# A conditioned transformer block on one core: paired DMA transpositions, fewer waits, and a new instruction order

## The chip, the cores and the metric

The kernel runs on one core of a Trainium2 chip. The core has a matrix engine (TensorE, PE in the profile), three engines for elementwise work (VectorE or DVE, ScalarE or ACT, GpSimd or POOL), a queue engine (SyncE or SP) and 16 DMA engines that all queues share. The metric is device time in microseconds (us) of one launch, lower is better. The times quoted for a kernel are the median of several runs.

## What is computed

The input x has 2048 rows of 640 features. A conditioning row c gives six vectors (two shifts, two scales, two gates) through one matrix product. The block is an attention over a sliding window of 256 keys with 32 heads of 20 features, then a gated MLP of width 1536, each behind a layer norm that is scaled and shifted, and each added to its input through a gate:

```python
def _A_ref(x, wqkv, wo):
    qkv = (x @ wqkv).reshape(B, S, 3, H, Dh)      # S = 2048, H = 32, Dh = 20
    scores = einsum('bhqd,bhkd->bhqk', q, k) * Dh ** (-0.5)
    mask = (i - j >= 0) & (i - j < 256)
    o = einsum('bhqk,bhkd->bhqd', softmax(where(mask, scores, -1e9)), v)
    return o.reshape(B, S, D) @ wo                # D = 640
def _B_ref(x, w_gate, w_up, w_down):
    return (sigmoid(x @ w_gate) * (x @ w_up)) @ w_down

sa, ca, ga, sb, cb, gb = (silu(c) @ w_mod).reshape(6, D)
x = x + ga * _A_ref(layernorm(x) * (1 + ca) + sa, wqkv, wo)
x = x + gb * _B_ref(layernorm(x) * (1 + cb) + sb, w_gate, w_up, w_down)
```

Inputs, weights and result are bf16.

## The kernel before

The 2048 rows are cut into 8 chunks of 256 rows, and a chunk into two blocks of 128. For each chunk the kernel runs these stages.

- `ln1` (L874): the statistics and the normalised rows `x` of both blocks, then their transposition into the tile `hT` (features on the partitions), then the scale and shift of `modulate` (L813). Chunks 0 and 1 are transposed on PE (`pe_transposes`, L831, for chunks below `NPH` = 2), the others by DMA (`transp_dma`, L808), one DMA of 128x640 for each block.
- `qkv` (L917): for each block, Q and then K are projected on PE (five matmuls of 320 columns for each half of the features) and copied by ACT or DVE out of PSUM into a staging tile `stg` of 128x1024, in which each head has 32 columns. The staging tile is then transposed into `QT` or `KT`. For chunks below `NPQ` = 2 PE does that, as matmuls with the identity (`M<-ident,stg` in the profile, four for each half) and a second copy out of PSUM; for the others one DMA transposition does it for each block and each of Q and K. There are four staging tiles. V is projected last.
- `attention` (L1175): for each half of the heads, sets of score matmuls into the one PSUM tile `S`, an exponential on ACT from `S` into `E`, masks on POOL, and one burst of matmuls of `E` with V, then a normalisation on DVE.
- `outproj` (L1213): the product with wo, the residual, the second layer norm, and its transposition into `h2T`, by DMA for all chunks, one DMA for each block.
- `mlp` (L1261): gate and up matmuls over `h2T` with 256 columns, a tanh on ACT, the product on DVE, then the down matmuls and the store.

The stages of different chunks are interleaved. While the weights are loaded (all through the same DMA queues, over the first quarter of the run) the conditioning vectors are made by small matmuls (`silubc` in the profile).

The order of all work is written out in `PLAN` (L353), a table of one number for each operation: the operation's place in the recording, and its engine. `Prog.schedule` (L151) walks the table, gives each operation to its engine in that order, and picks the buffer for each tile. `Prog.emit` (L262) then finds for each operation the semaphores that it must wait for. An operation waits for each operation that it depends on, also where an earlier wait of the same engine, or a wait that the awaited operation itself had made, already implies that it has ended. It skips a semaphore only where the same engine has waited for that value itself.

So each engine runs a fixed list. If the head of a list waits, everything behind it on that engine waits too. The DMA transpositions are all issued by SP.

Of the kernel before, what the change touches and what calls it, by code (L numbers as in the profile page):

```python
# [13 lines left out]
D = 640  # L14
H = 32
DH = 20
# [35 lines left out]
class Tile:  # L52
# [18 lines left out]
    @property  # L71
    def ap(self):
        return self.pool.aps[self.slot]

# [6 lines left out]
class Prog:  # L81
# [180 lines left out]
    def emit(self):  # L262
# [26 lines left out]
        for e in ENGS:  # L289
            cnt = 0  # L290
            for o in self.order[e]:
                if o.isdma:
                    continue
                if o.signal:
                    cnt += 1
                    o.key, o.val = e, cnt
        handles = {}
# [10 lines left out]
        with nc.Block() as block:  # L308
            for e in ENGS:
# [4 lines left out]
                def body(engine, ops=ops, e=e):  # L314
                    seen = {}
                    for o in ops:
                        w = {}
                        for d in need[o]:
                            if seen.get(d.key, 0) < d.val and w.get(d.key, 0) < d.val:
                                w[d.key] = d.val  # L320
                        for k, v in w.items():
                            engine.wait_ge(h(k), v)
                            seen[k] = v
# [5 lines left out]
                    if e == "sp":  # L329
                        for k, v in finals.items():  # L330
                            if seen.get(k, 0) < v:
# [17 lines left out]
def c_pe(n):  # L349
# [1026 lines left out]
```

## Time and profile before

| | |
|---|---|
| three runs | 324.90, 325.63 and 331.31 us; median 325.63 us |
| the profiled execution | 323.86 us, of which 321.8 us are the span from the first to the last instruction; 2.06 us lie around it |
| granted PE clock | 1.000 |
| busiest engines | PE 315.8 us, ACT 213.6 us, DVE 198.6 us, POOL 189.0 us |
| DMA | 32.96 MB in 62127 packets, of which 45946 are under 512 bytes |

The profile gives times as starts within the span and as durations. Matmuls overlap: a row's duration of one matmul is longer than the step from it to the next. The profile's step is therefore read from the starts of rows that follow each other. An arrow `<-` in brackets names what ended an idle time.

### The profile page before, as it was taken

To read this page: it belongs to the slowest core of one execution; us is meant where nothing else is said; L and a number is where in the kernel's file an instruction comes from. 1 tells how busy PE (TensorE), PEld (TensorE's weight loads), DVE (VectorE), ACT (ScalarE), POOL (GpSimd) and SP (SyncE) were. 2 spreads that over 40 slices of the span, in tenths; PEclk is the share of its full clock that TensorE was granted. 3 is DMA by queue.
4 is the path that set the end of the run, shared out by engine and by line. 5 is a ranking of instruction groups with operands and counts; after the bars stand their busy time and mean duration, and the time that the engine had idled before them with its cause. 6 is when DMAs were issued, how large, how long until landed. Compare 5 with 4: busy or idle time off the path is not lost.

```text
span 321.8 us, 11856 instructions
## 1 busy us (share of the span) xinstructions
PE 315.8 (98%) x5045; PEld 236.9 (74%) x5045; DVE 198.6 (62%) x424; ACT 213.6 (66%) x229; POOL 189.0 (59%) x349
## 2 busy tenths in 40 slices
PE   7999999999999999999999999999999999999997
PEld 2677667677877777766777677877877777877885
DVE  4689897877886756584555555465534474386323
ACT  2699897876787986768686867676976746411220
POOL 4338759778768483948484848577575826601000
PEclk9999999999999999999999999999999999999999
DMA  7989999999912534226327200220800006002101
GB/s 232 350 269 287 219 182 237 207 223 306 202 29 43 88 77 55 44 63 108 77 22 92 51 22 3 65 42 25 132 16 4 22 22 104 22 2 61 44 0 44
DMA packets 62127, 32.96 MB, mean 102 GB/s; under 512 B 45946, under 2 KB 60794, under 8 KB 62074
## 3 DMA queue, kind: packets, MB, share of 16 engines
q1 hardware_dynamic: 59904, 29.73, 43.5%
q10 hardware_dynamic: 2170, 2.46, 2.4%
q8 instruction: 40, 0.66, 0.9%
q14 instruction: 13, 0.11, 0.1%
HBM read 18.68 MB, written 2.62 MB: 66 GB/s over the span
## 4 chain that ended last, share of the span: by engine, by line
PE 93%; DMA 3%; DVE 1%; ACT 1%; issue 0%; ACTq 0%; DVEq 0%
PE M L686 77%; PE S L687 8%; PE M L687 7%; DMA hT<-x 2%; DMA x<-in_A_x_dram 1%; PE S L686 1%; ACT hT L819 1%; DVE st L781 1%; PE S L678 0%; DVE x L803 0%; ACT stg L902 0%; DVE KT L903 0%; ACTq L572 0%; DVE st L783 0%; ACT hT L902 0%
## 5 line engine op out<-in xcount | busy, mean ns | idle before, releaser
L1055 ACT ACTIVATE E<-S 128x2048 bf16<-128x2048 f32 x56 | 105.1, 1876 | 41.7 <-PE S L687 38.7
L1060 POOL TENSOR_SCALAR_AFFINE_SELECT E<-E 128x256 bf16<-128x256 bf16 x112 | 46.4, 424 | 57.4 <-ACT E L1055 24.6
L1064 POOL TENSOR_SCALAR_AFFINE_SELECT E<-E 128x512 bf16<-128x512 bf16 x112 | 70.3, 643 | 4.6 <-DVE x L803 1.2
L686 PE MATMUL M<-h2T,wg 128*128 128x256 bf16 x480 | 67.0, 273 | 0.0
L686 PE MATMUL M<-h2T,wu 128*128 128x256 bf16 x480 | 66.7, 273 | 0.0
L1277 DVE SCALAR_TENSOR_TENSOR hh<-sig,M 128x512 bf16<-128x512 f32 x48 | 32.4, 677 | 42.9 <-ACT sig L1275 25.2
L686 PE MATMUL M<-wd,hh 128*128 128x320 bf16 (+2 forms) x396 | 57.0, 295 | 0.0
L686 PEld LDWEIGHTS M<-h2T,wg 128*128 128x128 bf16 x480 | 45.4, 98 | 7.7 <-DVE T L1150 0.2
L686 PEld LDWEIGHTS M<-h2T,wu 128*128 128x128 bf16 x480 | 45.2, 98 | 7.3
L1275 ACT ACTIVATE sig<-M 128x512 f32<-128x512 f32 x48 | 28.5, 595 | 31.5 <-PE M L686 31.2
L686 PEld LDWEIGHTS M<-wd,hh 128*128 128x128 bf16 x396 | 37.2, 98 | 13.6 <-DVE hh L1277 0.2
L1033 POOL TENSOR_SCALAR_AFFINE_SELECT E<-E 128x1024 bf16<-128x1024 bf16 x28 | 31.9, 1145 | 4.7 <-ACT E L1029 3.2
L687 PEld LDWEIGHTS S<-QT,KT 20*64 20x64 bf16 (+1 forms) x1856 | 20.0, 100 | 17.0 <-issue 9.1
L687 PE MATMUL S<-QT,KT 20*64 20x256 bf16 (+5 forms) x1856 | 32.3, 228 | 0.1
L1029 ACT ACTIVATE E<-S 128x2048 bf16<-128x2048 f32 x14 | 26.3, 1876 | 7.2 <-PE S L687 7.1
L781 DVE BATCH_NORM_STATS2 st<-x 128x6 f32<-128x320 bf16 x64 | 28.9, 480 | 1.9 <-DMA x<-in_A_x_dram 1.5
L1150 DVE STREAM_TRANSPOSE T<-M 128x512 f32<-128x512 f32 x32 | 21.5, 700 | 13.3 <-PE S L687 11.7
L686 PE MATMUL M<-wk,hT 128*128 128x320 bf16 x160 | 27.9, 299 | 0.0
L1296 DVE TENSOR_TENSOR x<-M,x 128x320 bf16<-128x320 f32 (+2 forms) x33 | 15.4, 476 | 18.8 <-PE M L686 18.6
L686 PE MATMUL M<-wq,hT 128*128 128x320 bf16 x160 | 26.2, 299 | 0.6 <-DVE hT L820 0.5
L686 PE MATMUL M<-wv,hT 128*128 128x320 bf16 x160 | 26.1, 299 | 0.0
L686 PE MATMUL M<-wo,oT 128*128 128x320 bf16 x160 | 25.9, 299 | 0.0
(84 smaller groups left out, 356.7 us busy)
## 6 DMA issues: line engine op xcount, KB each, us to landing
x<-in_A_x_dram SPq DMA_DIRECT2D x18, 160.0 KB, 3.5
wd<-in_w_mod_dram SPq DMA_DIRECT2D x6, 320.0 KB, 5.4
wd<-in_B_w_down_dram SPq DMA_DIRECT2D x4, 480.0 KB, 5.6
wu<-in_w_mod_dram SPq DMA_DIRECT2D x5, 320.0 KB, 4.5
x<-in_A_x_dram ACTq DMA_DIRECT2D x8, 160.0 KB, 2.6
out_dram<-x SPq DMA_DIRECT2D x8, 160.0 KB, 1.9
wu<-in_B_w_up_dram SPq DMA_DIRECT2D x2, 576.0 KB, 5.6
wg<-in_B_w_gate_dram SPq DMA_DIRECT2D x2, 576.0 KB, 6.2
```

Of the source, the lines that this page charges most:

```text
L686: return e.matmul(o, l, r, start=st, stop=sp, skip_group_check=True)
L687: return e.matmul(o, l, r, start=st, stop=sp, tile_position=tp, skip_group_check=True)
L781: A("dve", lambda e, g, bi=bi, j=j: e.bn_stats(v(bi * 12 + j * 6, 6), src[bi].ap[:, j * 320:(j + 1) * 320]), 0.48, reads=[src[bi].r()], wr ...
L1029: A("act", lambda e, eng: e.activation(cell().rearrange("p m (x c) -> p m x c", c=64)[:, :, 0:4:3, :], Sp.ap[:].rearrange("p j (k x c) -> ...
L1033: A("pool", lambda e, eng, c0=c0, pat=pat, base=base, cm=cm: e.affine_select(cell()[:, :, c0:c0 + 64], cell()[:, :, c0:c0 + 64], pattern=p ...
L1055: A("act", lambda e, eng: e.activation(part(0, 512), Sp.ap[:], ACT.Exp, scale=SM_SCALE), 1.876, reads=[Sp.r()], writes=[E.r("C"), E.r("B") ...
L1060: A("pool", lambda e, eng, hc=hc, src=src, far_h=far_h: e.affine_select(side(hc), part(src, 64), pattern=[[0, 4], [-1 if far_h else 1, 64] ...
L1064: A("pool", lambda e, eng, c0=c0, near=near: e.affine_select(part(c0, 128), part(c0, 128), pattern=[[0, 4], [1 if near else -1, 128]], com ...
L1150: A("dve", lambda e, g, h=h: e.transpose(T1.ap[:, 512 * h:512 * h + 512], X[h].ap), 0.694, reads=[X[h].r()], writes=[T1.r(h)], prio=3.5, t ...
L1275: A("act", lambda e, g, pg=pg, sg=sg: e.activation(sg.ap[:], pg.ap[:], ACT.Tanh, scale=0.5), c_act(512), reads=[pg.r()], writes=[sg.r()], ...
L1277: A("dve", lambda e, g, pu=pu, sg=sg, f0=f0: e.scalar_tensor_tensor(out=hh.ap[:, f0:f0 + 2, :], in0=sg.ap[:].rearrange("p (a b) -> p a b", ...
L1296: A("dve", lambda e, g, ps=ps, bi=bi, c0=c0, n=n: e.tensor_tensor(x1[bi].ap[:, c0:c0 + n], ps.ap[:, 0:n], x1[bi].ap[:, c0:c0 + n], op=ALU. ...
```

## The change

Four things are changed together.

**One transposition for a pair.** The two normalised blocks of a chunk now lie side by side in one tile of 128x1280, and one DMA transposes both; the tiles `hT` and `h2T` change their layout from feature tile, row to block, feature tile, row. Q and K of a block lie side by side in one staging tile of 128x2048, and one DMA transposes both into a joint tile `QK`. The number of DMA transpositions of `hT` goes from 12 to 6, of `h2T` from 16 to 8.

**Chunk 1.** `NPQ` goes from 2 to 1: Q and K of chunk 1 are transposed by DMA (one DMA for each block), and PE's 32 identity matmuls for them and their eight copies out of PSUM go. The transposition of chunk 1's `hT` stays on PE (`NPH` is 2 as before). Q and K have 14 DMA transpositions after, 24 before.

**Buffers.** `x0` and `x2` (before 4 and 2 tiles of one block) become one pool of 3 tiles of a pair. `hT` and `h2T` (2 and 2) become one pool of 4. Staging is 2 tiles of 2048 columns instead of 4 of 1024. `QT` (3) and `KT` (4) become 4 joint tiles. The row of c uses a part of the tile `mt`.

**Waits and order.** `emit` now follows the plan with what each engine knows to have ended, through the waits of the operations that it waited for as well, and leaves out a wait that follows from others. Instructions that only wait, counted in the two built programs, go from 174 to 14 on ACT, from 170 to 56 on DVE, from 89 to 62 on PE, from 89 to 26 on POOL and from 78 to 19 on SP. `PLAN` is a new table throughout; more of the loads may be issued by ACT. One line of it:

```diff
-    119, 53, 76, 3, 8, 297, 86, 84, 300, 305, 333, 270, 277, 99, 281, 48, 442, 335, 28, 437, 447, 94, 13, 287, 422, 427,
...
-NPQ = 2
-PQ = ()
+NPQ = 1
...
+class Part:
+    def __init__(self, tile, i, view):
+        self.tile, self.i, self.view = tile, i, view
+    def r(self, key=None):
+        return self.tile.r((self.i, key))
+    @property
+    def ap(self):
+        return self.view(self.tile.ap, self.i)
...
+        for code in PLAN:
+            o = self.ops[code // 5]
+            known = seen[o.eng]
+            last = {}
+            for d in need[o]:
+                if known.get(d.key, 0) < d.val and (d.key not in last or last[d.key].val < d.val):
+                    last[d.key] = d
+            waits[o] = {k: d.val for k, d in last.items()
+                        if not any(x is not d and after[x].get(k, 0) >= d.val for x in last.values())}
+            for d in last.values():
+                for k, v in after[d].items():
+                    known[k] = max(known.get(k, 0), v)
+            after[o] = dict(known)
...
-    p_x0 = sbpool("x0", 4, [128, D])
-    p_x2 = sbpool("x2", 2, [128, D])
+    p_x0 = p_x2 = sbpool("x0", 3, [128, 2 * D])
...
-    p_hT = sbpool("hT", 2, [128, NDT, CH])
-    p_h2 = sbpool("h2T", 2, [128, NDT, CH])
-    p_stg = sbpool("stg", 4, [128, 1024])
-    p_QT = sbpool("QT", 3, [128, NG, CH])
-    p_KT = sbpool("KT", 4, [128, NG, CH])
+    p_hT = p_h2 = sbpool("hT", 4, [128, 2, NDT, 128])
+    p_stg = sbpool("stg", 2, [128, 2048])
+    p_QK = sbpool("QK", 4, [128, 2 * NG, CH])
...
-            turned[a] = [transp_dma(lambda bi=bi: t.ap[:, :, bi * 128:(bi + 1) * 128], lambda bi=bi: src[bi].ap[:], 4, 0.29,
-                                    [src[bi].r()], [t.r(("t", bi))], 1.42, f"atr{a}") for bi in range(2)]
+            turned[a] = [transp_dma(lambda: t.ap[:].rearrange("p b k c -> p (b k) c"), lambda: src[0].tile.ap[:], 4, 2 * TRH,
+                                    [src[bi].r() for bi in range(2)], [t.r(("t", bi)) for bi in range(2)], 1.45, f"atr{a}")]
...
-                else:
-                    transp_dma(lambda dst=dst, bi=bi: dst.ap[:, :, bi * 128:bi * 128 + 128], lambda s=s: s.ap[:], 3, 0.87,
-                               [s.r(0), s.r(1)], [dst.r((bi, 0)), dst.r((bi, 1))], 1.45, f"qkt{a}")
+            if a >= NPQ:
+                transp_dma(lambda bi=bi: qk.ap[:, :, bi * 128:bi * 128 + 128], lambda sqk=sqk: sqk.ap[:], 3, 2 * TRQ,
+                           [sqk.r((n, h)) for n in range(2) for h in range(2)],
+                           [qk.r((n, (bi, h))) for n in range(2) for h in range(2)], 1.55, f"qkt{a}")
...
-            for bi in range(2):
-                transp_dma(lambda bi=bi: h2.ap[:, :, bi * 128:(bi + 1) * 128], lambda bi=bi: x2[bi].ap[:], 2, 0.29,
-                           [x2[bi].r()], [h2.r(("t", bi))], 1.42, f"btr{a}")
+            transp_dma(lambda: h2.ap[:].rearrange("p b k c -> p (b k) c"), lambda: x2[0].tile.ap[:], 2, 2 * TRH,
+                       [x2[bi].r() for bi in range(2)], [h2.r(("t", bi)) for bi in range(2)], 1.45, f"btr{a}")
...
                 pairs = [(lambda kt=kt, i=i, ps=ps, w=w, f0=f0: (
-                    ps.ap[:, i * CH:(i + 1) * CH], w[:, kt, (f0 + i) * 128:(f0 + i + 1) * 128], h2.ap[:, kt, :]))
+                    ps.ap[:, i * CH:(i + 1) * CH].rearrange("p (b c) -> p b c", b=2), w[:, kt, (f0 + i) * 128:(f0 + i + 1) * 128],
+                    h2.ap[:, :, kt, :]))
```

The last lines show that the MLP's moving operand is now read as two pieces of 128 columns instead of one of 256. In the listings below, `M` and `S` are PSUM tiles, a name with a digit is one buffer of a pool, and the helper line that records a matmul is L686 or L687 before and L712 or L713 after.

**PE, from the first attention burst to the first scores of chunk 1.** Before, the identity matmuls that turn chunk 1's Q and K (`M<-ident,stg`) stand between the other work up to the first scores of the chunk (the first row with 64x256):

```order
L686 MATMUL M<-ident,stg 128x128 x8
L687 MATMUL S<-QT,KT 128x128 x16
L686 MATMUL M<-ident,stg 128x128 x4
L686 MATMUL M<-wk,hT 128x320 x5
L686 MATMUL M<-wv,hT 128x320 x7
L686 MATMUL M<-ident,stg 128x128 x4
L687 MATMUL S<-QT,KT 64x256 x8
L687 MATMUL S<-QT,KT 64x192 x8
L687 MATMUL S<-QT,KT 64x64 x8
L686 MATMUL M<-ident,stg 128x128 x4
```

After, the last projection of chunk 1's second Q ends three matmuls and one set of eight score matmuls ahead of these rows (the three are the last `M<-wq,hT` of chunk 1), and the last row is the first use of chunk 1's `QK`:

```order
L712 MATMUL M<-wv,hT 128x320 x13
L713 MATMUL M<-wu,silubc 32x160 x40
L713 MATMUL M<-E,V 32x256 x16
L713 MATMUL M<-E,V 32x128 x16
L713 MATMUL S<-QK 128x128 x16
L712 MATMUL M<-wv,hT 128x320 x5
L712 MATMUL M<-wq,hT 128x320 x2
L712 MATMUL M<-wk,hT 128x320 x2
L712 MATMUL M<-wq,hT 128x320 x5
L712 MATMUL M<-wk,hT 128x320 x3
L712 MATMUL M<-wv,hT 128x320 x5
L713 MATMUL S<-QK 64x256 x8
```

The identity matmuls are gone, and more of V's projections and the first projections of chunk 2 (the `wq` and `wk` rows) now stand ahead of chunk 1's first scores.

**SP, the first DMA transpositions.** Before, the first ones for Q and K are those of chunk 2, four DMAs for its two blocks, with loads between them:

```order
L810 DMA_TRANSPOSE hT1<-x00 128x5x128
L572 DMA gate19<-grow 4x160
L810 DMA_TRANSPOSE QT2<-stg1 128x8x128
L810 DMA_TRANSPOSE KT2<-stg2 128x8x128
L572 DMA x01<-in_A_x_dram 128x640
L572 DMA wg<-in_B_w_gate_dram 128x3x768
L572 DMA wd<-in_B_w_down_dram 128x3x640
L810 DMA_TRANSPOSE QT2<-stg0 128x8x128
L810 DMA_TRANSPOSE KT2<-stg3 128x8x128
```

After, the first for Q and K are chunk 1's, two DMAs, behind `hT` of chunks 2 and 3 and behind loads of the conditioning weights (`wu`, `wd`, `hh` from w_mod):

```order
L836 DMA_TRANSPOSE hT2<-x02 128x10x128
L593 DMA wu<-in_w_mod_dram 128x1280 x2
L593 DMA wo<-in_A_wo_dram 16x2x640 x2
L593 DMA wu<-in_w_mod_dram 128x1280
L593 DMA wo<-in_A_wo_dram 16x3x640
L593 DMA wu<-in_w_mod_dram 128x1280
L836 DMA_TRANSPOSE hT3<-x01 128x10x128
L836 DMA_TRANSPOSE QK1<-stg0 128x16x128
L836 DMA_TRANSPOSE QK1<-stg1 128x16x128
L593 DMA wo<-in_A_wo_dram 16x3x640
L593 DMA wd<-in_w_mod_dram 128x3x640
```

Fewer and larger transpositions stand in the queue, those of chunk 1's Q and K are new, and the last loads of the conditioning weights stand behind them.

**PE, the last chunk.** From the last product with wo to the first MLP matmul of the last chunk. Before (the row of 48 is the down product of chunk 6, the row behind it the first matmul over the last `h2T`):

```order
L686 MATMUL M<-wo,oT 128x320 x10
L686 MATMUL M<-wd,hh 128x320 x12
L686 MATMUL M<-h2T,wu 128x256 x6
L686 MATMUL M<-h2T,wg 128x256 x4
L686 MATMUL M<-h2T,wu 128x256 x2
L686 MATMUL M<-h2T,wg 128x256 x6
L686 MATMUL M<-h2T,wu 128x256 x6
L686 MATMUL M<-wd,hh 128x320 x48
L686 MATMUL M<-h2T,wg 128x256 x4
```

After:

```order
L712 MATMUL M<-wo,oT 128x320 x10
L712 MATMUL M<-hT,wg 128x256 x4
L712 MATMUL M<-hT,wu 128x256 x18
L712 MATMUL M<-hT,wg 128x256 x10
L712 MATMUL M<-hT,wu 128x256 x2
L712 MATMUL M<-wd,hh 128x320 x48
L712 MATMUL M<-hT,wu 128x256 x2
```

The 12 down matmuls and 24 MLP matmuls between the two have become 34 MLP matmuls.

More of the change, by code (lines that the diff above doesn't have):

```diff
@@ L296, in emit @@
                     o.key, o.val = e, cnt
+        seen = {e: {} for e in ENGS}
+        after = {}
+        waits = {}
+        for code in PLAN:
[11 more added lines that the diff above has]
+            after[o] = dict(known)
+            if o.key is not None:
+                after[o][o.key] = max(after[o].get(o.key, 0), o.val)
         handles = {}
@@ L314, in body @@
                 def body(engine, ops=ops, e=e):
-                    seen = {}
                     for o in ops:
[L317 to L321, printed above, removed]
+                        for k, v in waits[o].items():
                             engine.wait_ge(h(k), v)
-                            seen[k] = v
                         ins = o.fn(engine, e)
@@ L476 @@
 NPB = 0
+TRH = 0.45
+TRQ = 0.87
 OUTE = ("sp", "act")
```

69 lines of the change are left out of this document (39 added, 30 removed), and 216 rows, old and new, of the table PLAN.

## The prediction

> **What bounds the kernel now.** I read the page first: the busy shares, the slices and the chain that ended last.
>
> ```profile
> span 321.8 us, 11856 instructions
> PE 315.8 (98%) x5045; PEld 236.9 (74%) x5045; DVE 198.6 (62%) x424; ACT 213.6 (66%) x229; POOL 189.0 (59%) x349
> ...
> PE   7999999999999999999999999999999999999997
> ...
> PEclk9999999999999999999999999999999999999999
> DMA  7989999999912534226327200220800006002101
> ...
> PE 93%; DMA 3%; DVE 1%; ACT 1%; issue 0%; ACTq 0%; DVEq 0%
> ```
>
> PE is busy in 98% of the span, at full clock, and makes 93% of the chain; no other engine passes 66%. The DMA engines are full in the first ten slices (to 80 us) and have room later. A matmul's duration overlaps the next, so I checked the busy share by the step between rows of the timeline (start, duration, then the instructions):
>
> ```profile
> 23.59 0.39 PE L686 MATMUL M<-ident,stg 128*128 128x128 bf16 x4
> 23.81 0.43 PE L686 MATMUL M<-wk,hT 128*128 128x320 bf16 x2
> ...
> 149.71 0.43 PE L686 MATMUL M<-wv,hT 128*128 128x320 bf16 x2
> 149.98 0.43 PE L686 MATMUL M<-wk,hT 128*128 128x320 bf16 x2
> ...
> 290.44 0.82 PE L686 MATMUL M<-h2T,wu 128*128 128x256 bf16 x6
> 291.09 0.60 PE L686 MATMUL M<-h2T,wg 128*128 128x256 bf16 x4
> ```
>
> A matmul of 320 columns steps by 0.135 us (two in 0.27), one of 256 by 0.108 (six in 0.65), one of 128 by 0.055 (four in 0.22). That is about 0.42 ns a column in all three, so there is no slack between them. Then all that PE waited for:
>
> ```profile
> PE S L667 <- DVE E L662: 1.3, 1, 1.3
> PE M L686 <- DVE x L803: 1.0, 1, 1.0
> PE M L687 <- ACT V L902: 0.6, 1, 0.6
> PE M L686 <- DVE hT L820: 0.5, 1, 0.5
> ...
> 11.40 2.78 PE L686 MATMUL M<-wq,hT 128*128 128x320 bf16 x17 [0.49 <-DVE hT L820]
> ```
>
> These are four waits of 3.4 us in all (the columns are the sum, the times and the longest), and three of them (2.8 us) end with the first projection at 11.4 us, in the last row. So the time is PE's own work, and it can change in two ways only: PE gets fewer matmuls, or PE waits.
>
> **The change part by part.**
>
> *Chunk 1's Q and K by DMA.* 32 identity matmuls go, at 0.055 us each: -1.8 us, all on the path. Their eight copies on ACT and DVE cost nothing now, since neither engine is the bound. All other matmuls stay in kind and number.
>
> The Trainium skill (VectorE: DVE Perf Modes, The three transpose paths) gives 390 ns for a 128x128 transposition on TensorE and 1309 ns on the DMA path. By its first figure the gain would be an estimated 12.5 us and the time 311.4 us; the rows at 23.59 and 23.81 show 55 ns in a stream, and the measurement decides.
>
> *The MLP's moving operand in two pieces.* The rows of the gate product show two operands side by side, `wd` read in one run of 160 columns and `hh` in five pieces of 32:
>
> ```profile
> 38.26 0.26 PE L687 MATMUL M<-wd,silubc 128*32 128x160 bf16 x4
> 38.33 0.26 PE L687 MATMUL M<-hh,silubc 128*32 128x160 bf16 x4
> 38.40 0.26 PE L687 MATMUL M<-wd,silubc 128*32 128x160 bf16 x4
> ```
>
> Both step by 0.07 us. Pieces cost nothing: 0.
>
> *Waits left out.* A wait on PE that does not hold costs nothing that the steps above show, and the one late wait that does hold is 0.6 us (`ACT V`). It hangs on ACT's list, which is new; between 0 and -0.6 I take -0.6, since V's projection now stands further ahead of its use. The 2.8 us at the start stand: that part of the list is as it was. On the other engines fewer waits bring nothing to PE.
>
> *Paired transpositions, their price.* A pair waits for its later half and is moved at once. The landing of single ones, in empty queues and in the full ones at the start:
>
> ```profile
> L810 SPq DMA_TRANSPOSE hT<-x x2: 1262/1286/1310, 28.8 to 30.2; - x2
> ...
> DMA to landing us min/median/max: 5.4/5.8/6.2
> ...
> L810 SPq DMA_TRANSPOSE h2T<-x x2: 1201/1214/1227, 98.1 to 99.4; - x2
> ...
> DMA to landing us min/median/max: 2.6/2.6/2.6
> ...
> L810 SPq DMA_TRANSPOSE KT<-stg x1: 1232/1232/1232, 104.1 to 104.1; - x1
> L810 SPq DMA_TRANSPOSE QT<-stg x1: 1282/1282/1282, 105.4 to 105.4; - x1
> ...
> DMA to landing us min/median/max: 3.1/3.1/3.2
> ```
>
> Five feature tiles land 2.6 us after issue, eight land after 3.1, so a tile more costs about 0.17 us. My estimates for empty queues are 3.5 us for a pair of `hT` (ten tiles) and 4.5 us for a Q and K (16). In the full queues a transposition landed 2.8 to 3.6 us later.
>
> *Chunk 1's second QK.* Here is the one place where the new DMA stands close before its use. What covers it is the work on PE from the end of the second Q's projection to the first scores of chunk 1. By the new order that is 35 matmuls of `wq`, `wk` and `wv`, two score sets, the gate product and one burst with V:
>
> ```profile
> 28.59 0.40 PE L687 MATMUL S<-QT,KT 20*128 20x256 bf16 x8
> 28.92 0.88 PE L687 MATMUL M<-wu,silubc 128*32 128x160 bf16 x40
> 29.62 0.83 PE L687 MATMUL M<-E,V 128*32 128x256 bf16 x32
> 30.39 0.62 PE L686 MATMUL M<-ident,stg 128*128 128x128 bf16 x8
> 30.97 0.40 PE L687 MATMUL S<-QT,KT 20*128 20x128 bf16 x16
> 31.31 0.40 PE L686 MATMUL M<-ident,stg 128*128 128x128 bf16 x4
> ...
> L903 DVE CAST stg<-M 128x320 bf16<-128x320 f32 x34 | 16.2, 480 | 12.3 <-PE M L686 12.2
> ```
>
> That is 35 x 0.135 + 0.33 + 0.70 + 0.77 + 0.34 = 6.9 us. Against it stand the last matmul (0.3 us, the 0.43 of two less a step), the copy (0.48) and the DMA (4.5): 5.3 us in empty queues, which leaves 1.6 us. The queues are not empty at that time. With the delay of the rows at 28.8 (2.8 to 3.6 us) PE would wait 1.2 to 2.0 us; with none, 0. The first QK has 22 matmuls and a score set more, 3.3 us. The wait grows beyond 2.0 us if the two pairs of `hT` ahead add their own time: ten tiles more than the two singles, at 0.17 us, are 1.7 us, so the upper end is 3.7. I take 1.0, nearer to the full queue's row but below it, because the list now puts large loads of w_mod behind QK1. Behind these two on SP stand those loads (`wd`), which before were used at 38.26: they can be late by some us without a loss. That SP issues 28 transpositions instead of 52, at 1.2 us each, only helps it.
>
> *`h2T` of each chunk.* In the last chunk the path from wo to the MLP can be seen by itself (start, duration):
>
> ```profile
> 288.81 1.79 PE L686 MATMUL M<-wd,hh 128*128 128x320 bf16 x12
> ...
> 293.93 0.44 DVE L803 TENSOR_SCALAR x<-x,st 128x640 bf16<-128x640 bf16 x1
> ...
> 297.06 1.09 POOL L828 TENSOR_SCALAR h2T<-h2T,scB,shB 128x256 bf16<-128x256 bf16 x2 [4.58 <-DMA h2T<-x]
> ...
> 299.57 0.60 PE L686 MATMUL M<-h2T,wg 128*128 128x256 bf16 x4
> ```
>
> From wo's end (288.8) to the landing are 8.2 us, and the first scaled tile comes about 0.6 later: 8.8 of 10.8 us. The pair leaves after the second block's normalisation (294.4) and lands by the estimate at 297.9, 0.9 us later. The new order covers 34 x 0.108 + 48 x 0.135 = 10.2 us, the need is 9.7: it just fits, 0. In chunk 0 the same path lies in the full queues, with more work over it; between 0 and the 2.8 us delay I take +0.2, as its cover is longer.
>
> *Buffers.* Both staging tiles are held by chunk 1's two DMAs until they land, so chunk 2's first Q cannot be copied out of PSUM before. I count this with the rival below, since it bites only if those DMAs are late.
>
> **Sum.** -1.8 - 0.6 + 1.0 + 0.2 = -1.2 us on the profiled execution of 323.86 us: 322.7 us. The median of the runs shown, 325.63 us, lies 1.8 us above that execution. On its scale I forecast 324.4 us, the same within 2% (319.1 to 332.1 us), which is about what a measurement can tell from no change.
>
> **The rivals.**
>
> *Late QK1 (26%), within 2%.* The DMA runs behind what the queue still holds, and PE stalls at chunk 1's first scores and, through the held staging tiles, at chunk 2's projections. For it: all slices to 80 us are full, and the rows at 28.8 took 5.4 to 6.2 us. Against it: 1.6 us of slack and the loads put behind. With 3.7 us at the scores and again up to 2.8 at chunk 0's `h2T`, the sum is -2.4 + 6.5 = +4.1 us: 329.7 us. [...]
>
> *The pair is late in every chunk (7%), slower by over 2%.* `h2T` lands 0.9 us later in each of eight chunks. If the new order has no cover left, PE pays 8 x 0.9 = 7.2 us, and with 3.7 for QK1 and -1.8 the sum is +9.1: 334.7 us. It decides once the path of 9.7 us exceeds the work between wo and the MLP; in the last chunk that margin is 0.5 us. Against it: in the middle chunks other work stands between.
>
> *Nothing waits (13%).* Every DMA is hidden and the late waits vanish: -1.8 - 0.6 = -2.4 us, 323.2 us. Even with all 3.4 us of waits gone it is -5.2 us, 320.4 us, which is still within 2%.
>
> *Fewer DMAs and waits change nothing (4%).* The transpositions carry the same bytes, so only -1.8 us and the measurement's scatter are left: 323.8 us.
>
> **How the numbers follow.** My forecast (a small gain, 322.5 to 326.5 us) has 50%, the rivals what stands beside them. The range takes in the two that gain more (to 320.5) and the late QK1 (to 329.7); above it lies the 7% case, and some scatter of the runs at either end. Faster by over 2% needs more than all waits and the identity matmuls together, 2%; slower by over 2% is the 7% case; the rest, 91%, is the same.
>
> **What would show it.** In the profile after, `M<-ident,stg` has 32 instead of 64, and PE's busy time falls by about 1.8 us. PE's waits show whether a row ends with `DMA QK` at about 37 us, and how long; none would show the rival of no waits, 3 us or more the late QK1. The landing of `QK` should be 4.5 us in empty queues and of `hT` pairs 3.5 us; if they are much longer, the pairs are slower than two singles. A wait of PE for `hT` at the first `wg` of several chunks would show the slow rival. I am wrong if PE's matmuls step slower, or if a wait appears on an engine that I counted as free.

## The result, and the profile after

The changed kernel takes 328.97 us (median of 6 runs, 325.99 to 331.19), the kernel before 324.78 us (median of 6): a ratio of 1.0113, with a 95% interval of 1.0082 to 1.0144 (it leaves out one disturbed run of each, so it is not that of the two medians). I forecast a small gain; it is a small loss, within the range and within 2%, but of the other sign. The profiled execution after is the fastest of its six runs, 325.99 us against 323.86 before.

From the page of the changed kernel, the span, the busy shares, two of the rows of 40 slices and the shares of the chain:

```profile
span 324.3 us, 11337 instructions
...
PE 315.1 (97%) x5013; PEld 235.0 (72%) x5013; DVE 195.2 (60%) x416; ACT 209.3 (65%) x218; POOL 194.8 (60%) x360
...
PE   7999897999999999999999999999999999999997
...
DMA  7999999999845282130740000251260002103001
...
PE 86%; DMA 4%; POOL 3%; DVE 3%; SPq 1%; ACT 1%; issue 1%; ACTq 0%; DVEq 0%
```

The span is 2.5 us longer although PE has 32 matmuls less. PE's share of the chain falls from 93% to 86%, and the slices at 32 and 49 us have an 8 and a 7 in PE's row. All of PE's waits (total, times, longest):

```profile
PE M L712 <- DMA QK<-stg: 1.7, 2, 1.4
PE S L693 <- DVE E L688: 1.3, 1, 1.3
PE S L713 <- DMA QK<-stg: 1.1, 1, 1.1
PE S L713 <- issue: 0.7, 1, 0.7
PE M L712 <- DVE x L829: 0.5, 1, 0.5
PE M L712 <- issue: 0.4, 1, 0.4
PE M L712 <- POOL hT L854: 0.4, 1, 0.4
PE S L713 <- ACT E L1087: 0.2, 1, 0.2
```

The one late wait of before (`ACT V`) is gone. The wait at the first projection is still there, now named `issue` (0.45 us at 11.30 us), and so are the early ones for `DVE E` and `DVE x`. The others are new. Where they are, the timeline says (start, duration; the idle time and its releaser in brackets):

```profile
38.65 0.32 PE L713 MATMUL S<-QK 20*64 20x256 bf16 x8 [1.14 <-DMA QK<-stg]
...
50.15 0.43 PE L712 MATMUL M<-wq,hT 128*128 128x320 bf16 x2 [0.30 <-DMA QK<-stg]
...
54.21 0.30 PE L712 MATMUL M<-wq,hT 128*128 128x320 bf16 x1 [1.40 <-DMA QK<-stg]
...
75.92 0.20 PE L713 MATMUL S<-QK 20*128 20x64 bf16 x1 [0.73 <-issue]
...
110.49 0.28 PE L712 MATMUL M<-hT,wg 128*128 128x256 bf16 x1 [0.41 <-POOL hT L854]
```

The bracket leaves out the part of a stall that the matmul before covers. So for all runs below I use one measure: a stall is the step from one matmul's start to the next beyond its columns at 0.42 ns, counted if over 0.17 us, behind the start of the first projection (11.1 to 12.0 us). By it the five rows above are 1.30, 0.47, 1.56, 0.88 and 0.56 us. All stalls sum to 6.28 us after and 1.27 us before. The span's 2.5 us are then -1.8 (identity matmuls) + 5.0 (stalls) - 0.1 (an earlier first projection), and what is left, -0.6, lies in steps too short to count.

The profile explains 2.1 us of the 4.2 between the medians. In three of the six runs after, the mean granted clock is 0.995; of the 86 runs of the kernel before beside the experiments, one shows that. The last section comes back to that.

### The profile page after: what moved, and what is told of

Same layout as the page of the kernel before. It is cut to its first block, busy times and chain, and to the rows that moved or that the text cites. A ratio compares the mean times of both kernels' runs of the same rounds, so it can differ in the third digit from the quotient of the medians.

```text
span 324.3 us, 11337 instructions
## 1 busy us (share of the span) xinstructions
PE 315.1 (97%) x5013; PEld 235.0 (72%) x5013; DVE 195.2 (60%) x416; ACT 209.3 (65%) x218; POOL 194.8 (60%) x360
## 4 chain that ended last, share of the span: by engine, by line
PE 86%; DMA 4%; POOL 3%; DVE 3%; SPq 1%; ACT 1%; issue 1%; ACTq 0%; DVEq 0%
PE M L712 72%; PE S L713 7%; PE M L713 6%; DMA QK<-stg 2%; POOL E L1132 1%; DMA wo<-in_A_wo_dram 1%; DVE st L807 1%; DMA x<-in_A_x_dram 1%; SPq L593 1%; POOL hT L854 1%; ACT E L1087 1%; ACT E L1061 1%; SPq L836 1%; PE S L712 1%; POOL x L826 0%
## 5 line engine op out<-in xcount | busy, mean ns | idle before, releaser
L1092 POOL TENSOR_SCALAR_AFFINE_SELECT E<-E 128x256 bf16<-128x256 bf16 x112 | 45.3, 419 | 45.2 <-ACT E L1087 13.8
L712 PE MATMUL M<-hT,wu 128*128 128x256 bf16 x480 | 67.3, 273 | 0.0
L712 PE MATMUL M<-hT,wg 128*128 128x256 bf16 x480 | 65.6, 273 | 0.4 <-POOL hT L854 0.4
L712 PE MATMUL M<-wd,hh 128*128 128x320 bf16 (+2 forms) x396 | 57.8, 295 | 0.0
L712 PEld LDWEIGHTS M<-hT,wg 128*128 128x128 bf16 x480 | 45.5, 98 | 8.0 <-POOL hT L854 0.6
L712 PEld LDWEIGHTS M<-hT,wu 128*128 128x128 bf16 x480 | 45.1, 98 | 7.9
L712 PEld LDWEIGHTS M<-wd,hh 128*128 128x128 bf16 x396 | 37.3, 98 | 13.5 <-issue 0.2
L713 PE MATMUL S<-QK 20*64 20x256 bf16 (+5 forms) x1856 | 32.3, 228 | 2.3 <-DMA QK<-stg 1.1
L713 PEld LDWEIGHTS S<-QK 20*64 20x64 bf16 (+1 forms) x1856 | 20.0, 100 | 19.8 <-issue 7.2
L712 PE MATMUL M<-wq,hT 128*128 128x320 bf16 x160 | 27.3, 299 | 2.2 <-DMA QK<-stg 1.7
L712 PE MATMUL M<-wk,hT 128*128 128x320 bf16 x160 | 27.8, 300 | 0.0
L712 PE MATMUL M<-wv,hT 128*128 128x320 bf16 x160 | 26.8, 299 | 0.0
L932 DVE CAST stg<-M 128x320 bf16<-128x320 f32 x37 | 17.5, 482 | 14.0 <-PE M L712 13.8
L712 PE MATMUL M<-wo,oT 128*128 128x320 bf16 x160 | 25.9, 299 | 0.0
```

The costliest lines, as they stand in the source:

```text
L712: return e.matmul(o, l, r, start=st, stop=sp, skip_group_check=True)
L713: return e.matmul(o, l, r, start=st, stop=sp, tile_position=tp, skip_group_check=True)
L932: return e.tensor_copy(dst(), src())
L1092: A("pool", lambda e, eng, hc=hc, src=src, far_h=far_h: e.affine_select(side(hc), part(src, 64), pattern=[[0, 4], [-1 if far_h else 1, 64] ...
```

## The experiments

All are edits of one of the two kernels, measured beside runs of the kernel before on the same chip. The table comes first, since the text goes by it. "To 60 us" are the stalls of the profile where chunk 1's to 3's Q and K are projected, turned and first used; "exps" three stalls ahead of score sets at 59 to 67 us (the one that is long enough to be named waits for an exponential on ACT); "62 to 82" those that mostly no semaphore ends; the rest are 0.56 at 110 us, 0.23 at 160 us and a few early ones. The stalls are those of one profiled run, the median is that of all runs; stretches at a lower clock (last section) are not in the stalls.

| kernel | median us | ratio to before | all stalls | to 60 us | exps | 62 to 82 |
|---|---|---|---|---|---|---|
| before | 324.78 | 1 | 1.27 | | | |
| after | 328.97 | 1.0113 [1.0082, 1.0144] | 6.28 | 3.57 | 0.83 | 1.08 |
| e1 no hold | 329.20 | 1.0145 [1.0091, 1.0199] | 7.95 | 3.90 | 0.80 | 2.47 |
| e2 old waits | 329.70 | 1.0161 [1.0134, 1.0188] | 9.25 | 4.29 | 0.81 | 3.35 |
| e3 Q, K single | 331.33 | 1.0186 [1.0134, 1.0237] | 9.52 | 3.80 | 0.81 | 4.13 |
| e4 chunk 1 on PE | 328.37 | 1.0110 [1.0088, 1.0133] | 6.29 | 4.43 | 0.83 | 0.24 |
| e15 the same, later | 328.78 | 1.0119 [1.0088, 1.0151] | 7.09 | 5.22 | 0.84 | 0.24 |
| e8 hT single | 327.56 | 1.0089 [1.0063, 1.0116] | 7.25 | 5.40 | 0.80 | 0.24 |
| e16 third staging | 329.25 | 1.0159 [1.0124, 1.0194] | 9.01 | 5.08 | 0.83 | 1.86 |
| e12 SP dose | 329.29 | 1.0142 [1.0104, 1.0180] | 8.85 | 5.36 | 0.83 | 1.87 |
| e9 one wo load | 325.06 | 1.0007 [0.9978, 1.0036] | 5.15 | 2.77 | 0.83 | 0.75 |
| e11 wo early, 12 | 325.97 | 1.0030 [1.0002, 1.0059] | 6.73 | 2.61 | 0.83 | 2.50 |
| e14 wo early, 7 | 329.36 | 1.0129 [1.0076, 1.0182] | 8.40 | 4.28 | 0.83 | 2.50 |
| e17 light w_mod | 327.58 | 1.0107 [1.0074, 1.0140] | 6.50 | 2.58 | 0.80 | 2.11 |
| e5 light, columns | 328.76 | 1.0153 [1.0099, 1.0207] | 6.53 | 3.80 | 0.83 | 0.82 |
| e13 light, rows | 326.63 | 1.0080 [1.0047, 1.0113] | 6.40 | 4.09 | 0.83 | 0.68 |
| e7 before, fewer waits | 323.55 | 0.9968 [0.9948, 0.9989] | 0.52 | | | |

My theory at the start was the staging tiles; the rivals were the joint DMA by itself, and the rest of the order.

**One part of the change at a time.** First PE's hold on the staging tile is taken away (the tile is then taken by the copy), then the old waits are put back, then Q and K are turned by a DMA each, then chunk 1 is turned on PE again.

```diff
-                             hold=[sqk, qk] + (pss if PAIR else []))
+                             hold=[qk] + (pss if PAIR else []))
```

> The changed kernel, but a projection of Q or K on PE no longer holds the staging tile; only the copy out of PSUM waits for it. Theory 1 (staging: PE waits in chunk 2's projections until chunk 1's joint DMAs give back the two large staging tiles, 0.4 + 1.4 us of DMA QK in front of wq): these two waits go, PE's waits for DMA QK fall from 2.8 us to the 1.1 us in front of the scores, and the time falls by 1.5 to 2 us (ratio to before about 1.005). Theory 2 (the joint DMA itself is slower than two) and theory 3 (the new order or the waits left out): no change by this edit, ratio stays near 1.011, since the copy waits as long and blocks ACT or DVE and PSUM in its place.

The waits of PE on `DMA QK` at 50 and 54 us go, and others take their place: 0.74 us at 44 us for a copy, 1.40 at 48 us for an exponential. The sum to 60 us is 3.90 us, and the time is no better, as the rivals had it. Releasing the tile from PE does not release the copy.

```diff
-                        for k, v in waits[o].items():
+                        w = {}
+                        for d in need[o]:
+                            if seen.get(d.key, 0) < d.val and w.get(d.key, 0) < d.val:
+                                w[d.key] = d.val
+                        for k, v in w.items():
...
```

> The changed kernel with the waits written as before (none left out because others imply it). Theory 3a (leaving out waits matters): the time moves by 1 us or more either way. Theories 1 and 2: the same time within 0.3%, ratio to before near 1.011, since a wait that is already fulfilled showed no price.

It is not faster (1.0161), so nothing here makes leaving waits out a part of the loss. The other side shows it better: the kernel before with this one part alone.

> The kernel before with one part of the change alone: the waits that others imply are left out, order and tiles as before. By the prediction's steps at most -0.6 us: 324.2 to 324.8. If leaving waits out lets engines start early and so crowds the queues (a rival for the loss), 1 us or more slower: 326 us.

All of PE's waits in it:

```profile
PE M L698 <- DVE x L815: 1.5, 1, 1.5
PE S L679 <- DVE E L674: 1.3, 1, 1.3
PE M L698 <- DVE hT L832: 0.5, 1, 0.5
PE S L698 <- DMA wd<-in_w_mod_dram: 0.2, 1, 0.2
PE M L698 <- ACT stg L914: 0.2, 1, 0.2
```

The `ACT V` wait is gone, as the prediction took it, and the time is 1.0 us less, more than expected, with an interval that lies below 1. The order is that of before, so this does not need the new order. But the profiles of e10 and e18, controls that follow and that have the old waits, don't show the `ACT V` wait either; so the time is the evidence here, and not this row. It is the fastest complete version here, faster than both kernels.

```diff
-            if a >= NPQ:
-                transp_dma(lambda bi=bi: qk.ap[:, :, bi * 128:bi * 128 + 128], lambda sqk=sqk: sqk.ap[:], 3, 2 * TRQ,
...
+            for n in range(2) if a >= NPQ else ():
+                transp_dma(lambda bi=bi, n=n: qk.ap[:, NG * n:NG * n + NG, bi * 128:bi * 128 + 128],
+                           lambda sqk=sqk, n=n: sqk.ap[:, 1024 * n:1024 * n + 1024], 3, TRQ,
...
```

> The changed kernel, but each joint transposition of Q and K is two DMAs (Q, then K) at the same place of SP's list; buffers and order stay. Theory 2 (the joint DMA lands later than two singles): the waits for QK shrink and the time falls by 1 us or more. Theory 1: the staging tile comes back at the same time, since the bytes and the queue are the same, so the ratio stays at 1.011 within 0.3%, and a single lands 0.5 to 1.5 us before the joint one did.

Single ones gain nothing (1.0186, an interval that just overlaps that of the change), so the joint DMA is not at fault by being joint.

```diff
-NPQ = 1
+NPQ = 2
...
```

> The changed kernel, but chunk 1's Q and K are turned on PE again, the 32 identity matmuls and eight copies put back right behind the copies into the staging tile. PE's own work grows by 1.8 us. Theory 1: no DMA holds a staging tile before chunk 2 needs it and none feeds chunk 1's scores, so the waits for QK (2.8 us) go and the time falls by about 1 us net in the profile, more (2 to 4 us) where the runs were 328 to 330 us. Theories 2 and 3: 1.8 us slower or the same.

> The changed kernel with chunk 1's Q and K turned on PE again, as in the earlier run of this, but with the identity matmuls put six instead of three PE operations behind their copies, and all their copies on DVE, so that the two waits of 2.5 us which the earlier insertion made go. It takes 6.4 us of issuing from SP at 29 to 35 us and gives PE 1.8 us of matmuls back. If chunk 1's DMAs on SP are the main cost, SP's later transpositions leave 2 us or more earlier, the wait at 54 us goes too, and the time is 325 to 326.5 us in spite of the 1.8 us. If chunk 1's DMAs cost nothing beyond their own wait of 1.2, 328 to 330 us.

Both cost as much as the change. Each makes waits of its own (about 2.5 us for copies, of chunk 1's turned tiles too), which the second placing spread and did not remove, so they don't price chunk 1's DMAs. They do tell one thing: the wait at 54 to 55 us (1.56 and 1.99 us) stands without chunk 1's DMAs. It belongs to chunk 2's, and the projections that wait are chunk 3's.

```diff
-            turned[a] = [transp_dma(lambda: t.ap[:].rearrange("p b k c -> p (b k) c"), lambda: src[0].tile.ap[:], 4, 2 * TRH,
...
+            turned[a] = [transp_dma(lambda bi=bi: t.ap[:, bi, :, :], lambda bi=bi: src[bi].ap, 4, TRH,
...
```

> The changed kernel with hT and h2T turned by one DMA for each block again (28 instead of 14), in the same order. If pairs are late (the wait of 0.5 us at 110 us for h2T of chunk 1, hT ahead of QK1), 0.5 to 1 us of gain: 327.5 to 328.5. If SP's time of issue is the cost, 14 more issues at about 1.2 us, of which four stand ahead of chunk 1's and 2's Q and K, make those land up to 1 us later: 329.5 to 331.

With single ones the row of the MLP's wait is the same:

```profile
PE M L714 <- POOL hT L856: 0.4, 1, 0.4
```

The time fits the first expectation, its reason does not: the wait that the pair was to explain is unchanged, the stalls are not fewer, and the interval overlaps that of the change. So the pairs of `hT` and `h2T` cost nothing that shows here; the wait is for POOL's scaling.

**SP's time.** In the changed kernel SP's list at 27 to 50 us reads:

```profile
27.55 1.34 SPq L836 DMA_TRANSPOSE hT<-x  x1
28.99 6.41 SPq L836 DMA_TRANSPOSE QK<-stg  x2
35.45 0.84 SPq L593 DMA_DIRECT2D wo<-in_A_wo_dram  x1
...
44.74 0.42 SPq L593 DMA_DIRECT2D x<-in_A_x_dram  x1
45.26 4.94 SPq L836 DMA_TRANSPOSE QK<-stg  x2
```

The data of chunk 1's second QK are there at 30.9 us, by the last of these copies (30.40 and 0.49 us):

```profile
L932 DVE CAST stg<-M x4: 436/486/492, 26.9 to 30.4; 128x320 bf16<-128x320 f32 x4
L836 SPq DMA_TRANSPOSE QK<-stg x2: 2865/3184/3502, 29.0 to 32.5; - x2
```

The first takes SP 3.50 us, so the second leaves at 32.54, 1.65 us after its data. Chunk 2's second has its data at 45.1 us, leaves at 48.35 and lands at 54.07, and the stall ends at 54.21. Four versions change what SP has to issue.

```diff
-                dma(lambda j=j, x=x, t0=t0, t1=t1: wo[32 * j + 16 * x:32 * j + 16 * x + 16, t0:t1, :],
...
+    dma(lambda: wo[:, :, :], lambda: A_wo.rearrange("(t p) f -> p t f", p=128), 2.2, writes=list(R_wop.values()), prio=0.5,
...
```

> The changed kernel with `wo` loaded by one DMA instead of 16, with the same bytes but its rows in another order (so the attention's output projection is wrong). SP issues 13 loads fewer, about 6 us of its time, most of it between 23 and 51 us. New theory: PE's waits of 30 to 66 us come from SP's serial issuing. There chunk 1's second QK has its data at 30.9 us and is issued at 32.5, since the first takes 3.5 us to issue, and chunk 2's second is issued 3.2 us after its data. Then the waits at 38.7, 50 and 54 us (3.4 us) fall below 1 us: span about 321.5 to 322.5 and a median of 324 to 325. If full DMA queues are the cause, the same bytes keep the waits: 328 to 329 us.

> The kernel before with the same edit, as the control: its PE waits for no transposition, so by both theories 324 to 325 us.

The control is 323.86 us (0.9968 [0.9947, 0.9988]). The changed kernel goes from 1.0113 to 1.0007 (3.4 us), the control by 1.0 us. The time is near what SP's theory expected, the waits are not: that at the scores falls from 1.30 to 0.67 us, that at chunk 3's projection stays (1.69 us at 53.4 us, 1.56 before this edit), and all stalls fall by 1.1 us only. One of its ten runs has a clock of 0.995, against three of the change's six, which may be a part of the rest.

SP's list, with what is put into it:

```diff
+L593 DMA wo<-in_A_wo_dram x12
 L836 DMA_TRANSPOSE hT<-x 128x10x128
```

> The changed kernel, complete, with the 12 loads of `wo` that stand between SP's later transpositions issued ahead of its first one, where SP is idle from 18 to 21.5 us. If SP's issuing is the cause, chunk 1's and 2's QK leave up to 2 us earlier and the waits fall by 1 to 3 us: 325.5 to 327.5. The price: the first hT can leave 2 us later and land later behind these loads, which can cost up to 2 us at chunk 2's projections. By the rival (full queues, the same bytes) nothing is gained: 328 to 330 us.

From 1.0113 to 1.0030, 2.7 us less, and no row of PE's waits names `DMA QK`. The profiled run is one of its slowest, 329.61 us, with 2.11 us of wait for an exponential at 32.5 us (the price that the expectation named) and 2.30 us at 78 us; so its stalls do not explain the median. The same with seven:

> The changed kernel, complete, with only 7 of the `wo` loads moved into SP's idle time ahead of the first hT, so that this one isn't delayed (with 12 it left 2 us later). By the SP theory the second QK of chunk 1 leaves 1 to 1.5 us earlier and chunk 2's about 2 us earlier; the waits at 38.7 and 54 us fall by 1 to 2.5 us, with none at 32 us: 324.5 to 327. By the rival no gain: 328 to 330.

No gain; this one missed. SP took 3.89 us for chunk 1's first QK and 5.42 us for chunk 2's first, which landed 8.9 us after its issue. Moving loads moves their bytes too. So one run adds SP time and nearly no bytes:

```diff
+    scratch = dram("scratch", [4, 64])
+    for i in range(4):
+        dma(lambda i=i: scratch[i:i + 1, :], lambda: ident[0:1, 0:64], 0.05, reads=[R_ident], prio=1, tag="dose")
```

> The changed kernel with four tiny stores of 128 bytes added on SP between chunk 1's two QK transpositions: about 4 x 0.45 = 1.8 us of SP's time, and nearly no bytes. If SP's serial issuing is the cause, the second QK leaves at about 34.3 us instead of 32.5 and PE's wait at chunk 1's first scores grows from 1.2 to about 3 us; with all that is behind it on SP, 1.5 to 4 us slower: 330.5 to 333. If the queues' bytes are the cause, the wait stays at 1.2 and the time at 329 us.

SP's list in it:

```profile
29.50 3.51 SPq L837 DMA_TRANSPOSE QK<-stg  x1
33.06 1.36 SPq L594 DMA_DIRECT2D scratch<-ident  x4
34.47 3.10 SPq L837 DMA_TRANSPOSE QK<-stg  x1
```

The second QK leaves 1.9 us later; PE's wait at the first scores grows from 1.30 to 1.95 us (I expected 3) and the stalls to 60 us from 3.57 to 5.36. The profiled span is 2.8 us longer, but the ratio rises by only 0.003 (0.9 us), with intervals that overlap: the profile agrees with SP's time as a cause, the time does not decide.

**The bytes in the queues.** Two versions of the changed kernel load less of the MLP's weights, and one loads less of w_mod, ahead of chunk 1's transpositions; the kernel before with the same left out is the control.

```diff
-            dma(lambda k=k, m=m: dst[:, k:m, :], lambda k=k, m=m: src[:, k:m, :], work * (m - k), writes=Rs[k:m],
+            n = 32 if tag in ("wu0", "wu1") and m < 5 else dst.shape[2]
+            dma(lambda k=k, m=m, n=n: dst[:, k:m, 0:n], lambda k=k, m=m, n=n: src[:, k:m, 0:n], work * (m - k), writes=Rs[k:m],
...
```

> The changed kernel with most of the bytes of the MLP weights `wu` and `wd` not loaded (only 32 columns of most pieces, so the MLP's output is wrong); every DMA stays in number and place. These loads fill the queues from about 51 to 82 us. If the loss comes from transpositions, staging tiles and instruction fetches that stand in full queues, the stalls of PE at 54 us (1.6) and 76 us (0.9) go and the spread of the runs with them: about 324 us for the median, 322 us or less of span in the profile; the wait at chunk 1's first scores (1.2 at 38.7 us) stays, since it lies ahead of these loads. If the loss lies in the new order itself, whatever the queues hold, the time stays at 328 to 329 us.

> The kernel before with the same bytes left out, as the control. It has 1.1 us of waits after the first projection in all, so at most 1 us can go: 323.8 to 324.8 us by every theory. What tells them apart is the difference to the changed kernel with the same bytes left out: below 0 if full queues are the cause, about 4 us if the order is.

The control is 324.08 us (0.9983 [0.9970, 0.9997]). The changed kernel with narrow pieces stays at 328.76 us, where 324 was expected if full queues are the cause; but they did not empty the queues, so this does not decide. From 70 to 76 us (PE, PEld, DVE, ACT, POOL, granted clock, DMA share, GB/s), first the changed kernel, then this one, then the next with 4 of 128 partitions instead of narrow columns:

```profile
70.00:76.00 6.00, 5.27 (x142) 3.73 (x139) 5.70 (x12) 3.99 (x7) 2.84 (x7) 1.00 1.06 288
```

```profile
70.00:76.00 6.00, 5.81 (x146) 4.10 (x143) 5.08 (x11) 4.32 (x7) 3.29 (x8) 1.00 1.04 263
```

```profile
70.00:76.00 6.00, 5.82 (x146) 4.11 (x143) 5.08 (x11) 4.32 (x7) 3.29 (x8) 1.00 1.03 280
```

```diff
+            n = 4 if tag in ("wu0", "wu1") and m < 5 else 128
...
```

> The changed kernel with most of `wu` and `wd` left out by rows: 4 of 128 partitions of most pieces, so that few packets are left (the MLP's output is wrong). The same count of DMAs. It repeats the question of the narrow loads, since those left the DMA engines' busy share at 70 to 76 us as it was. If the stall of 0.9 us at 76 us, which no semaphore explains, comes from full queues, it goes: under 0.3 us, and with it the stretches at half clock in other runs: 326.5 to 328. The waits of 38 to 54 us stay by the SP theory. If it stays with free queues, it is something else.

Here the median is 326.63 us, in the expected range, but the ratio of 1.0080 is not clear of that of the change (the intervals overlap); and the stall at 76 us falls from 0.88 to 0.48 us, not to nothing. But the DMA share in that stretch is as it was (1.03), so that full queues make this stall is not shown.

```diff
+            n = 4 if tag == "wm1" and k > 0 else 128
...
-                    src = wm_ap[i][:, kt, c0:c0 + D]
+                    src = wm_ap[i][:, 0 if i == 1 else kt, c0:c0 + D]
```

> The changed kernel with four of the five pieces of w_mod's second load (`wu`, 327 KB each, issued by SP from 23 to 26 us) cut to 4 of 128 partitions, and the first piece read in their place (so B's shift and A's gate are wrong); as many DMAs as before. 1.3 MB less stand ahead of chunk 1's transpositions. If the full queues are the root (late landings, long issues on SP, staging tiles that come back late), chunk 1's QK are issued in about 2 us each and land in about 4.5, and the waits of 38 to 57 us (3.6) fall below 1.5 us: 325 to 326.5 us. If the order on SP and the engines is the root, whatever is in the queues, the waits keep their sum and the time is 328 to 329.5.

> The kernel before with the same bytes left out, as the control: no wait on PE of over 1 us depends on these loads, so 324 to 324.8 us.

The control is 323.96 us (0.9998 [0.9972, 1.0024]). Chunk 1's two QK in the light one:

```profile
L837 SPq DMA_TRANSPOSE QK<-stg x2: 2172/2482/2792, 29.0 to 31.2; - x2
```

The first takes SP 2.17 us instead of 3.50, the second leaves at 31.2 instead of 32.5, and the stall at chunk 1's first scores is 0.25 us instead of 1.30. So what the queues hold lengthens the issue and delays the landing, and with that the wait at the scores is explained. At chunk 3's projections 0.68 us for `DMA QK` and 1.22 us for `DVE wo` stand, the median of 327.58 us lies between the two expectations, and the ratio of 1.0107 is that of the change: this wait alone is not the loss.

**The staging tiles once more.**

```diff
+    p_stgx = Pool("stgx", [hhall[:, 0:2048]])
...
-            sqk = Tile(p_stg, f"s{a}_{bi}")
+            sqk = Tile(p_stgx if (a, bi) == (2, 1) else p_stg, f"s{a}_{bi}")
...
```

> The changed kernel, complete, with a third staging tile for one block: chunk 2's first one is staged in memory that the MLP does not use until about 76 us (two short memsets more on POOL). Chunk 2's second block and chunk 3's first then find a tile that came back long before. The wait of 1.6 us at 54 us has stayed at 1.0 to 2.5 us in most runs, with chunk 1 on PE too, so the staging tiles are its cause if it now goes: 326.5 to 327.5 us, the wait at chunk 1's first scores (1.2) unchanged. If something behind it (copies, exps, SP) bounds this place as when the hold was taken away, another wait of 1 us or more stands at 44 to 58 us and the time stays at 328 to 329.5.

PE's waits with the third tile begin:

```profile
PE S L718 <- DMA QK<-stg: 1.5, 1, 1.5
PE S L718 <- issue: 1.5, 1, 1.5
PE S L718 <- ACT E L1068: 1.4, 1, 1.4
...
PE M L717 <- DMA QK<-stg: 0.9, 1, 0.9
```

One staging wait is left of two (1.09 us at 56.3), PE waits 1.59 us for an exponential at 49 us, and the time is no better. My first theory falls in its simple form: more room, or a later hold, only moves the waits between 38 and 60 us.

## Why the prediction was wrong, point by point

- **Identity matmuls, -1.8:** right in the count, 32 instead of 64:

```profile
L712 PE MATMUL M<-ident,stg x32: 219/219/230, 12.9 to 21.4; 128*128 128x128 bf16 x32
```

  Busy time fell by 0.7 us, not by the 1.8 that I named as a sign: durations overlap, and the steps count.
- **The MLP's operand in two pieces, 0:** right; 18 matmuls of 256 columns take 1.96 us (292.29 to 294.25), 0.109 us each.
- **Waits left out, -0.6:** right in size, not in reason. Alone it gives -1.0 us (0.9968 [0.9948, 0.9989]) in the old order, so V's projection did not have to stand further ahead, and it is more than the one wait was worth. Where the rest comes from, the profiles don't show.
- **Chunk 1's second QK, +1.0:** right in place and size (1.30 us at 38.65 us, and 0.25 with light queues), right in cause by half. The second transposition starts 1.65 us after its data, since SP still issues the first, which the sum did not have; the scores start 6.1 us after that, so the landing took at most 1.6 us more than the 4.5 of empty queues, where the row that I used has 2.8 to 3.6. I looked at the loads of w_mod behind it; those ahead of it are what lengthens SP's issue (3.50 us, and 2.17 with four of them cut to 4 of 128 partitions).
- **"Buffers", counted "only if those DMAs are late":** this step failed. Chunk 3's projections wait 0.47 and 1.56 us. It is not chunk 1's DMAs that hold the tiles but chunk 2's, which I did not cost: they leave 3 us apart and land 4.8 and 5.7 us after issue. The sum has 0 for these 2.0 us, and they alone turn the forecast of -1.2 us into a loss.
- **"That SP issues 28 transpositions instead of 52, at 1.2 us each, only helps it":** this step failed with it. The price was that of 8 tiles:

```profile
L836 SPq DMA_TRANSPOSE QK<-stg x14: 1845/2693/4668, 29.0 to 235.0; - x14
...
DMA to landing us min/median/max: 4.4/5.6/6.9
```

```profile
L836 SPq DMA_TRANSPOSE hT<-x x14: 1253/1342/2311, 21.5 to 296.0; - x14
...
DMA to landing us min/median/max: 3.4/3.9/5.0
```

  A joint QK holds SP for 2.69 us at the median, and the second of a chunk cannot leave sooner. The code's list reckons with 1.55 (the last number of `transp_dma` in the diff). The shortest landings, 4.4 and 3.4, agree with my estimates of 4.5 and 3.5 for empty queues; in the full ones it was the issue, not only the landing, that grew.
- **`h2T`, +0.2:** 0.56 us at chunk 1's MLP, on POOL's account; the last chunk just fits, as forecast.
- **What I had no term for:** 0.83 us of stalls ahead of score sets at 59 to 67 us, the same in nearly every version of the new order, and the stall at 76 us with what follows it (1.08 us). The new order was costed only where the change touched it.

The three terms at nothing make 3.9 us (2.0, 0.8 and 1.1), about what lies between the forecast of -1.2 us and the span's +2.5.

Of the rivals the late QK1 (26%, 329.7 us) comes nearest in time, but by luck: its price was 3.7 us at the scores and 2.8 us at chunk 0's `h2T`, where 1.30 us and nothing were found, and the "3 us or more" that would show it did not come. It is right in that staging tiles can stop projections; they were chunk 2's tiles and chunk 3's projections, and the rival gave them no price.

What is shown: the wait at chunk 1's first scores goes by SP's time and by the queues' bytes. It grows with SP's time (1.95 us in e12, against 1.30 in the change and 1.52 to 1.70 in e1, e13 and e16, which leave this part of SP's list as it is) and nearly goes with fewer bytes (0.25 us in e17). The waits at 50 and 54 us end when chunk 2's DMAs have landed (50.0 and 54.1 us), and the one at 54 stands without chunk 1's DMAs (e4, e15). The form of the DMA (e3), the hold (e1), a third tile (e16) and the old waits (e2) gain nothing. The time falls clear of noise in e9 and e11 only, where hardly any of `wo`'s loads stand between SP's transpositions. That SP's list makes most of the loss fits this and is not shown: e14, with seven loads moved, gained nothing, and in e9 one staging wait stayed. What else stays open: how much is SP's time and how much the bytes, since the runs that part them (e12, e14, e17) agree only in part; and what makes the stall at 76 us.

## What to carry to other kernels

Price a DMA transposition three times: for the queue that issues it, for the landing, and for the buffer that it holds, each with the row of the same size in queues as full as there. Where PE is at 98%, an order in which everything just fits has no slack for 1 us of delay: what is gained in matmuls is paid back in waits, and mending one wait shows the next. Try each part of a change alone: the one without a cost (fewer waits) gave 0.3%, and the rest took it back more than four times over.

## What the runs showed of the hardware

Around some of PE's stalls the clock drops. The stall at 78 us of the run with seven early loads (start, duration), and the granted clock in the run with twelve, stretch by stretch (the columns as above; the clock is the last but two):

```profile
75.75 0.41 PE L714 MATMUL S<-QK 20*128 20x64 bf16 x31
78.30 0.23 PE L714 MATMUL S<-QK 20*128 20x64 bf16 x1 [2.14 <-issue]
```

```profile
28.00:33.70 5.70, 3.75 (x39) 2.28 (x39) 2.94 (x9) 4.42 (x6) 4.76 (x9) 1.00 1.14 334
33.70:37.10 3.40, 3.40 (x52) 2.26 (x54) 1.48 (x3) 2.09 (x3) 3.30 (x6) 0.50 1.18 237
37.10:41.00 3.90, 3.90 (x74) 2.82 (x62) 3.33 (x7) 2.75 (x4) 0.88 (x2) 1.00 0.96 206
78.10:81.50 3.40, 3.37 (x17) 2.42 (x17) 0.73 (x2) 2.00 (x2) 1.57 (x3) 0.50 0.77 271
```

PE runs at half clock for 3.4 us, which costs 1.7 us: more than many a stall itself. In the profiles it begins near the end of stalls of 1.96 to 2.66 us (seven times, from 0.4 us ahead of the end to 1.2 us behind it), not of each such stall (not of those of 2.1 us at 37 us in e2 and of 2.5 at 53 us in e14), and of none of 1.95 us or less. One such stretch in 327 us makes a mean clock of 0.995, which three of the six runs after show. That is a part of the loss that the profile of the fastest run does not have, and one reason why the runs spread; the run of 328.78 us has a clock of 1.000, so it is not the only one. The Trainium skill (TensorE: Matmul & The Clock Gate, Part 1: The HAM clock gate) tells of free-running windows of about 3.4 us and of half clock after an idle one. The length of the stretches agrees; but here stalls of 2.0 us were enough, less than a window, and the measurement decides.

The stall at 76 us stands ahead of the last of a set of 32 score matmuls, with no semaphore to wait for (`issue`). Eleven profiles have it, with 0.5 to 2.7 us. The packets of the traces tell when it ends. One queue of the page is named `instruction`:

```profile
q8 instruction: 39, 0.64, 0.8%
```

Its packets are of 16 KB, and in all eleven profiles the stall ends 1.29 to 1.53 us after one of them has landed, whatever its length. In e4, e8 and e15 there is no such stall, and the packet landed 4.4, 1.4 and 4.1 us ahead of the same matmul; in e1 1.65 us stand behind the set instead (named `DVE Tn`) and end 1.55 us after the packet. This fits instructions of PE that come late, and it is argued only: no run moved this packet alone, so the cause stays open.
